# Induced-set attention with a squared-ReLU layer on one core: the first batch's opening redone, and the last batch's second-attention scores made three groups at once

## The chip, the cores and the metric

One core of one Trainium2 chip runs the whole program. The metric is device time in microseconds (us) of one execution; three executions of the kernel before are shown, and their median counts. Engines are named as the profile names them: PE (matmul; PEld is its weight load), DVE, ACT, POOL and SP (which issues the DMAs).

## What is computed

Four batches of 12480 tokens with 128 channels go through a two-step attention over 32 inducing points, and every token's result through a layer of 2048 hidden units. Cut to what matters:

```python
def mab(q, kv):
    s = scale * (q @ kv.transpose(0, 2, 1))
    s = s - s.max(-1, keepdims=True)
    a = np.exp(s)
    a /= a.sum(-1, keepdims=True) + 1e-09
    return a @ kv
h = mab(I, x)            # 32 points look at all tokens of a batch: "scores" and "values"
y = mab(x, h)            # every token looks at the 32 points: "attend"
r = np.maximum(y @ w_in, 0.0)
out = (s * (r * r) + b) @ w_out
```

All inputs are float32 in value; the two weight matrices arrive as float64 and are narrowed on the chip.

## The kernel before

**Units of work.** A block is 480 tokens, a group (`GR`) four blocks; a batch has 26 blocks in seven groups, 0 to 6, the last of two blocks. The hidden layer takes a block in eight pairs of 128 hidden units, so there are 832 pairs in all. `pair` (line 928 its matmuls) makes 256 hidden values for 480 tokens in one of three PSUM buffers `h`: two matmuls, with the second attention folded into the weights `wst` (w_in times h) and the block's attention weights `a2t`. ACT or DVE takes the ReLU (L942, L944), ACT its square rounded to the matmul's short format (`square`, L1010), DVE the exact square (L965), POOL or DVE the remainder (L987). `out_part` (L1035) then multiplies the two pieces with w_out's halves `w_hi` and `w_lo`, six matmuls a pair, into one of two PSUM banks `x`. The first eight pairs (`NATIVE`) instead take the plain float32 square and an unsplit `w_out_raw`: two float32 matmuls a pair.

**Attention beside it.** For each group of four blocks the second attention (`attend`) is one piece on PE (L799: four matmuls that lie side by side in the array), then a transpose, maximum, exponential, sum, product and transpose on DVE and ACT, and DMAs that spread the result into `a2t`. The next batch's first attention is made in the same time: `scores` (L701), `top`, `values` (L742). `visit` puts an `attend` and up to two groups of scores, or a piece of values, into PE's queue one directly behind the other, the scores' results into an `h` buffer; the tables `ATTEND_AT`, `SCORES_WITH`, `VALUES_WITH` and `VALUES_AT` say with which block. In batch 0 before, group 6 of batch 1's scores goes with the first visit, groups 0 to 5 with the next three, and the second piece of batch 1's values stands alone (`VALUES_AT`).

**The opening.** Batch 0's first attention has nothing to hide under. `load_first` brings its tokens (channel by token); `p1_unit` makes the scores (L480), exponential (L493), its transposes (L500) and the values (L511); the tokens that the values need the other way round are made by `turn_x`: eight transposes on PE (L453) and a copy (L214). Only group 5 comes turned from memory (`TURNED`, `load_turned`, 120 rows wide), into a buffer that an earlier group has to free. At the same time eight chunks of weights are loaded (`load_weight`) and narrowed (`narrow`: L331 to L348, five pieces on DVE, two on ACT), and w_out's chunks are split (`split_w_out`, L356). Then the 32 points' values are put together (`h_unit`, `h_out`, L609), the first block's attention is made in a short way (`attend_first`, its last step a cast into `a2t`), `w_first` makes `wst`, and the pairs begin.

**What sets the order.** The program is written by a planner (`Plan`): every step of every unit is a generator's `yield` of an engine, a cost and what it waits for; the planner picks by start time plus a weighted urgency, and the instructions stand in that order in each engine's queue. Constants and tables ahead of the class set it. Each queue runs strictly in order, so a step waits for all that stands ahead of it. The DMAs are all issued by SP, in the order of `ORDER` at first.

Of the kernel before, what the change touches and what calls it, by code (L numbers as in the profile page):

```python
# [19 lines left out]
P = 128  # L20
# [16 lines left out]
SLIP = 0.1744  # L37
WEIGHT = 0.0178
LEAN = {'ACT': -0.5309, 'DVE': 0.6608}
R_LEAN = {'DVE': -0.2301, 'ACT': -0.2128}  # L40


M_U = -5.8018
R_U = 4.5067
SQ = 1.1237
MM = 0.2134
S_U = -0.7565
C_U = -10.6897
OUT_HI = 3.9914
OUT = 0.2122  # L50
FRONT = -1.1612
FIRST = -200.0
SPREAD = 74.0965
FIRST_FRONT = 0.3289
SPLIT_U = 237.6882

NATIVE = 8
H_U = -10.6844
N_U = -24.7788
W_IN_U = -167.7494  # L60
W_OUT_U = 10.3457
W_URGENCY = 3.9038
W_STEP = 19.8754
# [7 lines left out]
RUN = 512  # L71
A_OFF = 19
# [8 lines left out]
TOP_AT = (17, 11, 11)  # L81
VALUES_WITH = (((), (), (), (), (0,), (2, 3)), ((), (), (), (0,), (1,), (2, 3)), ((), (), (), (0,), (1,), (2, 3)))
VALUES_AT = (((1, 20),), (), ())
# [7 lines left out]
VISIT_U = -14.4858  # L91
# [3 lines left out]
class Plan:  # L95
# [7 lines left out]
    def __init__(self):  # L103
        self.free, self.events, self.units, self.end, self.start = {}, {}, [], 0.0, 0.0
        self.eng, self.by = None, {}
# [4 lines left out]
    def _step(self, unit, urgency, ready, src):  # L110
        want = next(unit, None)
        if want is not None:
# [9 lines left out]
            waits = [w for w in waits if not isinstance(w, float) and w != "both"]  # L122
            self.units.append([unit, urgency + more, (ready, src), engs, waits, urgency, lean, None, both])
# [26 lines left out]
    def run(self):  # L150
        while self.units:
            able = {}
            for u in self.units:
# [10 lines left out]
                able.setdefault(eng, []).append((at + WEIGHT * urgency, at, engs[eng], u))  # L164
# [7 lines left out]
            at, _, u, self.eng = min(picks, key=lambda x: x[0])  # L172
            self.units.remove(u)
            self.start, self.end = at, at + u[3][self.eng]
# [7 lines left out]
def tile_attn_relu2(ctx: ExitStack, tc: tile.TileContext, xT, xH, xN, xQ, indT, w_in, w_out, s_rep, b_rep, outT):  # L182
# [13 lines left out]
    const = ctx.enter_context(tc.tile_pool(name="const", bufs=1))  # L196
    xt_pool = ctx.enter_context(tc.tile_pool(name="xt", bufs=XT))
# [13 lines left out]
    def copy(out, in_):  # L211

        if plan.eng == "ACT":
            nc.scalar.copy(out=out, in_=in_)  # L214
        else:
            nc.vector.tensor_copy(out=out, in_=in_)

# [22 lines left out]

    ind_sb = const.tile([P, M], F32, name="ind_sb")
# [5 lines left out]
    w_hi = const.tile([P, NF, P], F32R, name="w_hi")  # L247
    w_lo = const.tile([P, NF, P], F32R, name="w_lo")
# [26 lines left out]
    dma = [2.7]  # L275

    def landing(us, lag=3.0):

        dma[0] = max(dma[0], plan.end + lag) + us * (1.2 if dma[0] < 10.0 else 1.0)
        return dma[0]  # L280
# [4 lines left out]
    def load_xt(gate, b, g, use):  # L285
# [7 lines left out]
        xt_tiles[b, g, use] = t, n  # L293
# [16 lines left out]
    def load_weight(gate, name, c):  # L310
        turn, free = ring("g1", 4)
        yield "SP", 0.45, free, *gate
        sl = slice(c * WC, (c + 1) * WC)
        src, dst = (w_in, w_in_sb) if name == "w_in" else (w_out, w_out_raw.rearrange("p f d -> p (f d)"))
        raw = ew.tile([P, WC, 2], I32, name="g1", bufs=4)
        nc.sync.dma_start(out=raw.rearrange("p n w -> p (n w)"), in_=src[c].bitcast(I32))
        raws[name, c] = raw, turn
        plan.events["raw", name, c] = landing(1.3)
        plan.spawn(narrow((name, c), dst[:, sl], ("raw", name, c)), W_IN_U if name == "w_in" else W_OUT_U)
        if name == "w_out":  # L320
            plan.spawn(split_w_out(c), SPLIT_U)


    def narrow(name, dst, *waits):
        raw, turn = raws.pop(name)
# [15 lines left out]
        nc.vector.scalar_tensor_tensor(out=dst, in0=lo, scalar=2.0**-52, in1=dst, op0=ALU.mult, op1=ALU.add)  # L341
        yield "DVE", 0.62, "both"
# [962 lines left out]
```

## Time and profile before

| | us |
|---|---|
| median of three runs | 1551.88 (1550.89 to 1552.01) |
| the profiled execution, its own time | 1552.4 |
| its span, first to last instruction | 1550.6 |
| PE busy | 1542.8 (99%) |
| POOL busy | 1471.1 (95%) |
| ACT busy | 1482.0 (96%) |
| DVE busy | 1469.9 (95%) |

All four engines are busy nearly all the time, so a share does not tell which one holds the others up. That is read from the chain that ended last (PE has 96% of it), from PE's idle time in each stretch, and, in the opening, from what PE waits for. The profiled execution took 0.5 us more than the median.

### The profile page before, as it was taken

How to read it: one execution, taken by the hardware profiler on the slowest of the kernel's cores; microseconds unless marked ns; L12 is line 12 of the kernel's file. 1: busy time of each engine (PE TensorE's matmuls, PEld its weight loads, DVE VectorE, ACT ScalarE, POOL GpSimd, SP SyncE). 2: the span in 40 equal slices, each digit the busy share in tenths (PEclk: the TensorE clock that was granted, in tenths of full speed). 3: DMA queues.
4: the chain of work that ended last, by engine and by line, in shares of the span. 5: the costliest groups of instructions: out<-in, count | busy, mean ns of one | idle time of the engine just before them, and what ended most of it. 6: DMA issues, size and time to landing. Idle time of an engine off the chain costs nothing.

```text
span 1550.6 us, 24505 instructions
## 1 busy us (share of the span) xinstructions
PE 1542.8 (99%) x8135; PEld 1294.9 (84%) x8135; DVE 1469.9 (95%) x1648; ACT 1482.0 (96%) x1750; POOL 1471.1 (95%) x665
## 2 busy tenths in 40 slices
PE   9999999999999999999999999999999999999999
PEld 6688888888888888888888888888888888888887
DVE  5999999999999999999999999999999999999998
ACT  7899999999999999999999999999999999999998
POOL 0299999999999999999999999999999999999998
PEclk9999999999999999999999999999999999999999
DMA  8212321332233123123232321321313112112100
GB/s 300 64 56 80 122 72 71 114 130 96 68 111 115 39 103 115 39 103 115 71 85 80 118 76 66 115 80 65 112 60 96 32 52 71 40 44 71 57 22 32
DMA packets 53482, 130.12 MB, mean 84 GB/s; under 512 B 11262, under 2 KB 37758, under 8 KB 53358
## 3 DMA queue, kind: packets, MB, share of 16 engines
q1 hardware_dynamic: 53358, 128.56, 25.2%
q8 instruction: 66, 1.08, 0.3%
q14 instruction: 58, 0.48, 0.1%
HBM read 74.50 MB, written 25.56 MB: 65 GB/s over the span
## 4 chain that ended last, share of the span: by engine, by line
PE 96%; DMA 2%; DVE 1%; POOL 0%; issue 0%; ACT 0%; SPq 0%; ACTq 0%; DVEq 0%; POOLq 0%
PE x L1035 68%; PE h L928 23%; PE x L799 2%; PE h L742 1%; PE h L701 1%; DMA g<-in_w_in_dram 1%; DMA xn<-in_xQ_dram 1%; DMA s_sb<-in_s_rep_dram 0%; DVE g L965 0%; POOL g L987 0%; PE h L651 0%; ACT xn L214 0%; PE x L742 0%; PE x L511 0%; SPq L420 0%
## 5 line engine op out<-in xcount | busy, mean ns | idle before, releaser
L987 POOL TENSOR_TENSOR g<-g,g 128x960 fp32r<-128x960 f32 x657 | 1469.8, 2296 | 73.6 <-DVE g L965 67.8
L1035 PE MATMUL x<-g,w_hi 128*128 128x480 f32 x3296 | 1063.6, 375 | 0.0
L1010 ACT ACTIVATE g<-r 128x960 fp32r<-128x960 f32 (+1 forms) x805 | 796.2, 1029 | 16.5 <-DVE r L944 2.4
L965 DVE SCALAR_TENSOR_TENSOR g<-h,r 128x960 f32<-128x960 f32 x657 | 739.4, 1146 | 22.4 <-ACT r L942 14.2
L1035 PEld LDWEIGHTS x<-g,w_hi 128*128 128x128 f32 x3296 | 614.8, 187 | 91.8 <-POOL g L987 3.3
L942 ACT ACTIVATE r<-h 128x960 f32<-128x960 f32 x660 | 622.8, 969 | 27.3 <-PE h L928 26.3
L1035 PE MATMUL x<-g,w_lo 128*128 128x480 f32 x1648 | 617.3, 375 | 0.0
L928 PE MATMUL h<-a2t,wst 128*128 128x480 f32 x1664 | 484.7, 378 | 0.7 <-DVE g L965 0.7
L928 PEld LDWEIGHTS h<-a2t,wst 128*128 128x128 f32 x1664 | 306.6, 187 | 65.4 <-DVE x L805 7.3
L1035 PEld LDWEIGHTS x<-g,w_lo 128*128 128x128 f32 x1648 | 308.9, 187 | 42.8
L944 DVE TENSOR_SCALAR r<-h 128x960 f32<-128x960 f32 x172 | 197.7, 1150 | 9.5 <-PE h L928 7.1
L987 DVE TENSOR_TENSOR g<-h,g 128x960 fp32r<-128x960 f32 x167 | 192.6, 1154 | 12.7 <-ACT g L1010 1.3
L965 DVE SCALAR_TENSOR_TENSOR h<-h,r 128x960 f32<-128x960 f32 x167 | 193.1, 1157 | 6.4 <-ACT r L942 5.7
L1044 ACT ACTIVATE ob<-x,bias 128x480 f32<-128x480 f32 x103 | 68.0, 660 | 4.1 <-PE x L1035 3.9
L799 PE MATMUL x<-xt,hT 128*32 128x480 f32 x208 | 28.3, 578 | 0.0
L805 DVE STREAM_TRANSPOSE x<-x 128x480 f32<-128x480 f32 (+1 forms) x28 | 19.3, 688 | 2.2 <-PE x L799 2.1
L742 PEld LDWEIGHTS h<-xn,eT 128*32 128x32 f32 (+1 forms) x570 | 17.0, 109 | 5.0 <-issue 4.8
L823 DVE STREAM_TRANSPOSE x<-x 128x480 f32<-128x480 f32 (+1 forms) x28 | 19.5, 696 | 0.9
L742 PE MATMUL h<-xn,eT 128*32 128x128 f32 (+1 forms) x570 | 19.6, 273 | 0.0
L821 DVE TENSOR_TENSOR x<-x,l 128x480 f32<-128x480 f32 (+1 forms) x28 | 18.5, 661 | 0.7
L701 PE MATMUL h<-xt,ind_sb 128*32 128x480 f32 x156 | 19.1, 566 | 0.0
L810 DVE TENSOR_TENSOR x<-x,mx 128x480 f32<-128x480 f32 (+1 forms) x28 | 18.4, 656 | 0.1
(147 smaller groups left out, 375.4 us busy)
## 6 DMA issues: line engine op xcount, KB each, us to landing
xt<-in_xT_dram SPq DMA_DIRECT2D x41, 960.0 KB, 5.5
out_dram<-ob SPq DMA_DIRECT2D x104, 240.0 KB, 2.0
a2t<-hl SPq DMA_DIRECT2D x412, 60.0 KB, 2.0
xn<-in_xN_dram SPq DMA_DIRECT2D x18, 512.0 KB, 6.1
xn<-in_xN_dram SPq DMA_DIRECT2D x18, 448.0 KB, 6.7
r<-in_xH_dram SPq DMA_DIRECT2D x7, 480.0 KB, 8.2
xt<-in_xT_dram SPq DMA_DIRECT2D x7, 480.0 KB, 5.4
wst<-hl SPq DMA_DIRECT2D x48, 64.0 KB, 2.0
```

The source lines that it names most:

```text
L701: nc.tensor.matmul(ps[M * q:M * (q + 1), 0:BLK], ind_sb, xt[:, q], start=True, stop=True)
L742: nc.tensor.matmul(ps[M * c:M * (c + 1), 0:P], eT[0:rows, n], xn_tiles[b, g, half][0][0:rows, n - half * TH], start=m < P // M, stop=m + P ...
L799: nc.tensor.matmul(ps[M * q:M * (q + 1), 0:BLK], hT[:, 0:M], xt[:, q], start=True, stop=True)
L823: nc.vector.transpose(out=s, in_=s)
L928: nc.tensor.matmul(h[:, u, 0:BLK], wst[:, c * P:(c + 1) * P], A, start=True, stop=True)
L942: nc.scalar.activation(out=r, in_=hv, func=AF.Relu)
L944: nc.vector.tensor_scalar(out=r, in0=hv, scalar1=0.0, scalar2=None, op0=ALU.max)
L965: nc.vector.scalar_tensor_tensor(out=g, in0=hv, scalar=0.0, in1=r, op0=ALU.max, op1=ALU.mult)
L987: eng.tensor_tensor(out=g2, in0=g, in1=hi.bitcast(F32), op=ALU.subtract)
L1010: nc.scalar.activation(out=q["g1_t"][:, sl, :], in_=q["r_t"][:, sl, :], func=AF.Square)
L1035: nc.tensor.matmul(o, w, g, start=first and n == 0, stop=left == 0 and n == len(ops) - 1)
L1044: nc.scalar.activation(out=ob, in_=o, func=AF.Identity, bias=bias, scale=1.0 if scaled else s_sb)
```

## The change

Batch 0's opening is redone in these ways. Group 6 too comes turned from memory, and both turned groups go to homes of their own (`turned_0` in the second weight tile's room, and the two `hl` buffers), so that their loads wait for nobody; the turned tokens are stored in memory with 128 rows, of which 120 are used. Six token tiles have homes by a table (`X_HOME`). The first super-block comes in two halves. The scores of three groups of batch 1 (6, 4, 5: `GAP`) are made in the opening, after the last values of batch 0, into banks that are free there; the first regular `attend` waits for the evacuation of two of them. w_out's raw chunks get buffers of their own (`w2`), which later hold the split halves in place of `w_hi` and `w_lo`; so the split of a half waits for its raw chunks to be used up, and for `s`, which is now loaded last. Of the narrowing, a piece that ACT did may go to POOL, for three chunks (`POOLED`) a DVE piece is replaced by one on ACT and one on POOL, and the last piece may go to POOL. The order of the loads is new.

The tables of batch 0 follow: the visits there carry scores of groups 0 to 3 only, and its values go with visits as in the other batches. In the last batch `turned_scores` makes the second-attention scores of groups 1, 2, 3 in one visit, and of 4, 5, 6 in another; the extra groups' scores are transposed into an SBUF tile, and their `attend` starts from there, with nothing on PE. All the planner's constants are other ones, and a table of urgencies for single steps (`URGENT`, 55 rows) is added; costs of many steps in the `yield`s are changed by hundredths.

```diff
-SLIP = 0.1744
-WEIGHT = 0.0178
+SLIP = 0.1762
+WEIGHT = 0.0161
...
-TURNED = (5,)
-ORDER = (
-    ("x", 0), ("x", 1), ("w_out", 0), ("x", 2), ("w_out", 1), ("x", 3), ("w_in", 0), ("x", 4), ("w_in", 1),
-    ("w_in", 2), ("x", 5), ("x", 6), ("w_out", 2), ("q", 5), ("w_in", 3), ("w_out", 3),
-)
-WARM = 6
+TURNED = (5, 6)
+X_HOME = (4, 1, 3, 0, 3, 2, 1)
+GAP = (6, 4, 5)
+ORDER = (('x', 0), ('w_in', 1), ('x', 1), ('x', 2), ('w_out', 2), ('w_out', 1), ('w_in', 0), ('w_out', 3), ('x', 3), ('x', 4), ('x', 5), ('x', 6), ('n', 6), ('q', 5), ('w_in', 2), ('q', 6), ('w_in', 3), ('n', 4), ('n', 5), ('w_out', 0), ('s', 0))
+POOLED = (('w_in', 2), ('w_out', 0), ('w_out', 2))
+WARM = 7
+URGENT = {
+    ('x', 3): -234.92,
...
+LAST_WITH = ((2, 3), (), (), (5, 6), (), ())
-SCORES_WITH = (((6,), (0, 1), (2, 3), (4, 5), (), ()), ((0, 1), (2, 3), (4, 5), (), (), ()), ((0, 1), (2, 3), (4, 5), (), (), ()))
+SCORES_WITH = (((), (0, 1), (2, 3), (), (), ()), ((0, 1), (2, 3), (4, 5), (), (), ()), ((0, 1), (2, 3), (4, 5), (), (), ()))
...
-VALUES_WITH = (((), (), (), (), (0,), (2, 3)), ((), (), (), (0,), (1,), (2, 3)), ((), (), (), (0,), (1,), (2, 3)))
-VALUES_AT = (((1, 20),), (), ())
+VALUES_WITH = (((), (), (), (0,), (1,), (2, 3)), ((), (), (), (0,), (1,), (2, 3)), ((), (), (), (0,), (1,), (2, 3)))
+VALUES_AT = ((), (), ())
...
     def load_weight(gate, name, c):
...
+        else:
+            yield "SP", 0.45, *gate
+            raw, used = w2_pool.tile([P, WC, 2], I32, name="w2"), ("raw used", c)
...
     def narrow(name, dst, *waits):
...
-        nc.scalar.activation(out=dst, in_=m, func=AF.Copy, scale=2.0**-20, bias=1.0)
+        yield dict(ACT=0.525, Pool=0.68), {"ACT": M_LEAN}, 0.0
+        if plan.eng == "ACT":
+            nc.scalar.activation(out=dst, in_=m, func=AF.Copy, scale=2.0**-20, bias=1.0)
+        else:
+            nc.gpsimd.tensor_scalar(out=dst, in0=m, scalar1=2.0**-20, scalar2=1.0, op0=ALU.mult, op1=ALU.add)
+        if name in POOLED:
+            yield "ACT", 0.525
+            nc.scalar.activation(out=m.bitcast(F32), in_=lo, func=AF.Copy, scale=2.0**-52)
+            yield "Pool", 1.37
+            nc.gpsimd.tensor_tensor(out=dst, in0=m.bitcast(F32), in1=dst, op=ALU.add)
+        else:
+            yield "DVE", 0.6, "both"
+            nc.vector.scalar_tensor_tensor(out=dst, in0=lo, scalar=2.0**-52, in1=dst, op0=ALU.mult, op1=ALU.add)
...
-        nc.vector.tensor_tensor(out=dst, in0=dst, in1=e.bitcast(F32), op=ALU.mult)
+        yield dict(DVE=0.6, Pool=1.37), 0.0, "both"
+        either().tensor_tensor(out=dst, in0=dst, in1=e.bitcast(F32), op=ALU.mult)
...
     def split_w_out(c):
...
+        yield "ACT", 0.615, "s", ("w_out", c), *[("raw used", n) for n in mine], ("w2", half - 1)
+        if half not in w2:
+            w2[half] = [w2_pool.tile([P, 2 * WC // P, P], F32R, name="w2") for _ in range(2)]
...
     def homes():
...
-            home["x", g] = g if g < 4 else 1 + (g - 4) % 3
+            home["x", g] = X_HOME[g]
...
+        for n in range(SB):
+            home["xQ", TURNED[0] * GR // SB + n] = turned_0[:, n * TH * P:(n + 1) * TH * P]
+        for g in TURNED[1:2]:
+            for n in range(SB):
+                t = p2.tile([P, 2, WC], F32, name="hl")
+                home["xQ", g * GR // SB + n] = t.rearrange("p a t -> p (a t)")
...
     def load_first(g):
...
+            step = SB if j else 1
+            for i in range(0, SB, step):
+                nc.sync.dma_start(out=t[:, a + i:a + i + step].rearrange("p q t -> p (q t)"), in_=xH[j, :, i * BLK:(i + step) * BLK])
...
     def load_turned(g):
...
-            yield "SP", 0.45, ("v done", j - 4)
-            nc.sync.dma_start(out=home["q"][j % 4], in_=xQ[j])
+            yield "SP", 0.45
+            nc.sync.dma_start(out=home["xQ", j], in_=xQ[j])
...
     def scores(b, g, ps, *waits):
...
-                "s": p1.tile([P, NG, BLK], F32, name="s"),
+                "s": st[0]["room"].rearrange("p (g t) -> p g t", g=NG) if b == 1 and GAP
+                else p1.tile([P, NG, BLK], F32, name="s"),
...
+    def turned_scores(b, g, ps, *waits):
+
+        rows = M * blocks_in(g)
+        yield "PE", 1.14, ("hT", b), ("x", b, g, 2), *waits
+        ps = ps()
+        scores_2(b, g, ps)
+        yield "DVE", 0.58
+        nc.vector.transpose(out=st[b]["s"][0:rows, g], in_=ps[0:rows, 0:BLK])
+        plan.set(("turned", b, g))
...
     def attend(b, g, ps, *waits):
...
+        ahead = b == B - 1 and any(g in gs for gs in LAST_WITH)
+        if ahead:
+            yield "DVE", 0.57, ("turned", b, g), *waits
+            ps = ps()
+            s = ps[0:rows, 0:BLK]
+            v = s.rearrange("p (n i) -> p n i", i=M)
+            t = st[b]["s"][0:rows, g].rearrange("p (n i) -> p n i", i=M)
...
     def front_work(blk_g):
...
-                    yield (*want, ("ob", blk_g - 1) if blk_g else "first") if first else want
+                    start = [("ob", blk_g - 1)] if blk_g else ["first", *[("scores", 1, g) for g in GAP[0::2]]]
+                    yield (*want, *start) if first else want
...
-            side = []
+            side = [(turned_scores, b, g) for g in LAST_WITH[n]] if b == B - 1 else []
...
     def opening():
...
-                if n == 1:
-                    nc.sync.dma_start(out=s_sb, in_=s_rep)
-                    nc.sync.dma_start(out=b_sb, in_=b_rep)
...
+            elif what == "n":
+                yield from load_xt((), 1, n, 1)
+                i = GAP.index(n)
+                plan.spawn(
+                    scores(1, n, (lambda: bank[1], lambda: hs[0][:, 0])[i % 2],
+                           ("p1", 0, NG - 1), *([("scores", 1, GAP[i - 2])] if i > 1 else [])),
+                    FIRST + GAP_U + i + urgent("n", n),
+                )
...
 def kernel(x, inducing, moe_w_in, moe_w_out, moe_s, moe_b):
...
+    xq = np.zeros((N // (SB * BLK), P, SB * NQ * C), x.dtype)
+    xq[:, :T] = x[0].reshape(N // (SB * BLK), SB, NQ, T, C).transpose(0, 3, 1, 2, 4).reshape(-1, T, SB * NQ * C)
```

PE's queue where the first pairs begin, before. `accb` with `hl` is the last matmul of the short first attention, `w_in_sb` is `w_first`, `a2t` with `wst` a pair, `hT` the first regular `attend`, `g` with `wst` the first native output piece.

```order
L875 MATMUL x0_85<-accb_101,hl_610 128x120 x4
L632 MATMUL h_114<-w_in_sb_92,hT_575 128x512
L1231 MATMUL h_112<-g2_115 128x320
L928 MATMUL h_627<-a2t_621,wst_587 128x480 x2
L928 MATMUL h_632<-a2t_621,wst_587 128x480 x2
L799 MATMUL x1_86<-xt_117,hT_575 32x480 x4
L928 MATMUL h_645<-a2t_621,wst_587 128x480 x2
L928 MATMUL h_649<-a2t_621,wst_587 128x480 x2
L928 MATMUL h_653<-a2t_621,wst_587 128x480 x2
L1035 MATMUL x0_85<-g_643,wst_111 128x480 x2
```

The same place after; `ind_sb` is a group of batch 1's scores.

```order
L834 MATMUL x1_89<-xt_379,ind_sb_92 32x480 x2
L1031 MATMUL x0_88<-accb_104,hl_614 128x120 x4
L1397 MATMUL h_116<-g2_90 128x480 x2
L1084 MATMUL h_636<-a2t_627,wst_602 128x480 x2
L760 MATMUL h_117<-w_in_sb_97,hT_584 128x512
L760 MATMUL h_118<-w_in_sb_97,hT_584 128x512
L834 MATMUL x1_89<-xt_454,ind_sb_92 32x480 x4
L1084 MATMUL h_659<-a2t_627,wst_602 128x480 x2
L930 MATMUL x1_89<-r_123,hT_584 32x480 x4
L1084 MATMUL h_673<-a2t_627,wst_602 128x480 x2
L1084 MATMUL h_677<-a2t_627,wst_602 128x480 x2
L1084 MATMUL h_683<-a2t_627,wst_602 128x480 x2
L1191 MATMUL x0_88<-g_665,wst_115 128x480 x2
```

Two pieces of `w_first` and one group of scores now stand between the first pair and the second. In both orders five pairs and one `attend` precede the first native output piece.

ACT's queue at the same place, before, from the cast into `a2t` to the first ReLU.

```order
L214 CAST a2t_621<-x0_85 128x480
L214 CAST wst_587<-h_114 128x512
L942 ACTIVATE r_635<-h_627 128x960
```

And after; `w2` with `s_sb` is a w_out chunk's upper half, `rebias` and `g2` are narrowing of the last w_out chunk.

```order
L279 CAST a2t_627<-x0_88 128x480
L458 ACTIVATE w2_632<-wst_115,s_sb_93 128x512 x2
L414 ACTIVATE g_630<-g_630,rebias_108 128x512
L279 CAST wst_602<-h_117 128x512
L422 ACTIVATE g2_639<-w2_457 128x512
L279 CAST wst_602<-h_118 128x512
L1098 ACTIVATE r_657<-h_636 128x960
```

Six pieces stand between the cast into `a2t` and the first ReLU, where one did.

PE's queue at the last batch's first visit of that kind, after; before, a single `attend` of four matmuls stood at each of three such places.

```order
L930 MATMUL x1_89<-xt_12372,hT_11969 32x480 x4
L930 MATMUL h_12658<-xt_12374,hT_11969 32x480 x4
L930 MATMUL h_12658<-xt_12376,hT_11969 32x480 x4
L1084 MATMUL h_12679<-a2t_12291,wst_12076 128x480 x2
```

The second and third group's scores go to an `h` buffer, which a pair would otherwise have.

## Rows read from the trace of the kernel before

**Rows 1.** Page, part 1: busy time, share of the span and instructions.

```profile
PE 1542.8 (99%) x8135; PEld 1294.9 (84%) x8135; DVE 1469.9 (95%) x1648; ACT 1482.0 (96%) x1750; POOL 1471.1 (95%) x665
```

**Rows 2.** Chain that ended last, one piece of it: start us, length us, what.

```profile
74.12 2.13 PE x L1035 x10
```

**Rows 3.** Timeline of PE, 0 to 50 us: start, length, engine, line, operation.

```profile
...
26.65 1.09 PE L453 MATMUL h<-ident,xt 128*120 128x128 f32 x8
27.67 1.01 PE L480 MATMUL x<-r,ind_sb 128*32 128x480 f32 x8
...
29.20 1.00 PE L480 MATMUL x<-r,ind_sb 128*32 128x480 f32 x4
...
35.21 1.74 PE L511 MATMUL x<-xn,eT 120*32 120x128 f32 x44 [1.07 <-DMA xn<-in_xQ_dram]
...
37.51 0.64 PE L609 MATMUL h<-s,sw 128*32 128x128 f32 x14 [0.25 <-DVE rl L595]
...
46.36 1.06 PE L928 MATMUL h<-a2t,wst 128*128 128x480 f32 x4
...
49.75 0.56 PE L1035 MATMUL x<-g,wst 128*128 128x480 f32 x1
```

**Rows 4.** Timeline of PE at five attention pieces in later stretches.

```profile
84.35 1.01 PE L799 MATMUL x<-xt,hT 128*32 128x480 f32 x8
...
86.09 0.70 PE L928 MATMUL h<-a2t,wst 128*128 128x480 f32 x2
...
143.16 1.01 PE L799 MATMUL x<-xt,hT 128*32 128x480 f32 x8
...
145.71 0.70 PE L928 MATMUL h<-a2t,wst 128*128 128x480 f32 x2
...
313.54 1.01 PE L799 MATMUL x<-xt,hT 128*32 128x480 f32 x8
...
316.22 0.69 PE L928 MATMUL h<-a2t,wst 128*128 128x480 f32 x2
...
346.88 0.38 PE L1035 MATMUL x<-g,w_hi 128*128 128x480 f32 x1
347.18 1.94 PE L742 MATMUL x<-xn,eT 128*32 128x128 f32 x60
349.05 0.91 PE L928 MATMUL h<-a2t,wst 128*128 128x480 f32 x3
...
1215.17 1.01 PE L799 MATMUL x<-xt,hT 128*32 128x480 f32 x8
1216.12 0.70 PE L1035 MATMUL x<-g,w_hi 128*128 128x480 f32 x2
```

**Rows 5.** Windows: length; busy PE, PEld, DVE, ACT, POOL; PEclk, DMA share, GB/s.

```profile
5.00:10.00 5.00, 5.00 (x39) 3.09 (x37) 0.81 (x2) 2.63 (x5) 0.00 (x0) 1.00 0.74 242
10.00:15.00 5.00, 4.99 (x60) 2.80 (x56) 1.59 (x4) 4.89 (x10) 0.00 (x0) 1.00 1.01 410
...
30.00:35.00 5.00, 3.86 (x57) 2.87 (x55) 3.82 (x12) 4.65 (x12) 0.00 (x0) 1.00 0.96 237
...
34.00:46.36 12.36, 10.79 (x101) 7.40 (x97) 9.98 (x28) 7.04 (x16) 0.00 (x0) 1.00 0.16 56
```

**Rows 6.** Groups by form, 0 to 46.36 us: busy us, mean ns | idle before.

```profile
L214 ACT COPY xn<-h 120x1024 f32<-120x1024 f32 x11 | 11.3, 1029 | 6.9 <-PE h L453 6.9
...
L637 DVE TENSOR_TENSOR wst<-h,wst 64x512 fp32r<-64x512 f32 x3 | 2.1, 694 | 0.1
...
L356 ACT ACTIVATE w_hi<-wst,s_sb 128x512 fp32r<-128x512 f32 x2 | 1.5, 738 | 0.0
```

**Rows 7.** Timeline of ACT, 45 to 50 us.

```profile
45.48 0.56 ACT L214 CAST a2t<-x 128x480 fp32r<-128x480 f32 x1 [0.33 <-DVE wst L341]
...
47.03 0.97 ACT L942 ACTIVATE r<-h 128x960 f32<-128x960 f32 x1
```

**Rows 8.** Page, part 5: POOL's group.

```profile
L987 POOL TENSOR_TENSOR g<-g,g 128x960 fp32r<-128x960 f32 x657 | 1469.8, 2296 | 73.6 <-DVE g L965 67.8
```

More of the change, by code (lines that the diff above doesn't have):

```diff
@@ new lines @@
+URGENT = {
+    ('x', 3): -234.92,
+    ('w_in', 1): 384.17,
+    ('w', 1): 32.13,
+    ('n', 4): -165.82,
+    ('w', 0): -64.56,
+    ('turn', 4, 0): 27.09,
+    ('turn', 2, 1): 149.29,
+    ('x', 1): 14.97,
+    ('v', 6): 132.81,
+    ('turn', 2, 0): 24.44,
+    ('x', 6): 23.68,
+    ('x', 4): 29.01,
+    ('v', 5): 30.4,
+    ('turn', 0, 0): -1.93,
+    ('turn', 4, 1): 107.18,
+    ('x', 0): 28.8,
+    ('w_in', 3): -107.28,
+    ('w_in', 2): -33.54,
+    ('w_out', 0): 54.0,
+    ('e', 2): -73.1,
+    ('a',): -91.2,
+    ('split', 0): -52.36,
+    ('n', 2): -145.64,
+    ('n', 1): -53.73,
+    ('v', 1): 116.75,
+    ('turn', 6, 1): -158.08,
+    ('n', 6): 31.77,
+    ('turn', 3, 1): -58.68,
+    ('w_out', 1): 2.74,
+    ('w_in', 0): 6.86,
+    ('e', 4): -22.03,
+    ('turn', 1, 0): -1.74,
+    ('split', 1): -56.02,
+    ('turn', 5, 0): -28.41,
+    ('turn', 1, 1): 7.37,
+    ('w_out', 2): -4.46,
+    ('h',): -28.6,
+    ('v', 3): 7.59,
+    ('e', 6): -15.74,
+    ('turn', 5, 1): -19.49,
+    ('n', 3): 5.58,
+    ('split', 3): -0.2,
+    ('x', 2): 0.98,
+    ('n', 5): 1.62,
+    ('n', 0): 40.51,
+    ('turn', 3, 0): 31.87,
+    ('w_out', 3): -50.52,
+    ('e', 3): 27.69,
+    ('w', 3): 59.87,
+    ('w', 2): -21.65,
+    ('e', 5): -27.4,
+    ('e', 1): -29.11,
+    ('v', 4): 3.57,
+    ('e', 0): 0.92,
+}
@@ L121, in _step @@
             more = sum(w for w in waits if isinstance(w, float))
-            waits = [w for w in waits if not isinstance(w, float) and w != "both"]
-            self.units.append([unit, urgency + more, (ready, src), engs, waits, urgency, lean, None, both])
+            kind = True if "tiled" in waits else False if "whole" in waits else None
+            waits = [w for w in waits if not isinstance(w, float) and w not in ("both", "tiled", "whole")]
+            self.units.append([unit, urgency + more, (ready, src), engs, waits, urgency, lean, None, both, kind])
     def extend(self, us):
@@ L392, in homes @@
     def homes():
+        for _ in range(XT):
+            ring("xt", XT)
         for _ in range(2):
-            ring("xt", XT)
             ring("r", 2)
@@ L462, in p1_unit @@
             d = st[0] = {
+                "room": room,
                 "mx": sm.tile([P, NG], F32, name="mx"),
@@ L683, in scores @@
         rows = M * nb
-        if b not in st:
+        if b not in begun:
+            begun.add(b)
+            yield "DVE", 0.15, *waits
             d = st[b] = {
@@ L1034, in out_part @@
         for n, (w, g) in enumerate(ops):
-            nc.tensor.matmul(o, w, g, start=first and n == 0, stop=left == 0 and n == len(ops) - 1)
+            nc.tensor.matmul(o, w(), g, start=first and n == 0, stop=left == 0 and n == len(ops) - 1)
         used()
@@ L1051, in out_part @@
         plan.set(("ob", blk_g))
+    turned_0 = wst_pool.tile([P, F], F32, name="wst")
+    turns = [j for j in range(NSB) if j * SB // GR not in TURNED]
     w_out_raw = wst_pool.tile([P, NF, P], F32, name="wst")
@@ L1169, in tile_attn_relu2 @@
             for f, *args in (args[0], *args[1]) if f is visit else ((f, *args),):
-                if f in (scores, attend):
+                if f in (scores, turned_scores) or f is attend and not any(args[1] in gs for gs in LAST_WITH if args[0] == B - 1):
                     fetch(first + n - AHEAD, load_xt, *args, 1 if f is scores else 2)
@@ L1191, in turn_work @@
         yield from turn_x(g, h, lambda: hs[turns.index(j) % 2], ("turn", before[turns.index(j)]))
-    turns = [j for j in range(NSB) if j * SB // GR not in TURNED]
     before = [-2, -1, *turns]
```

265 lines of the change are left out of this document (154 added, 111 removed).

## Prediction

> **What bounds the kernel now.** I read the page's busy shares first: four engines between 95% and 99% [rows 1], so shares alone settle nothing. The chain that ended last does: after the opening it is PE's own output matmuls, one row after another, and its steps are even, 2.13 us for ten matmuls, so 0.213 us each [rows 2]. From the first pair at 46.36 us [rows 3] to the end PE never waits long for anybody. So in that part a microsecond taken out of PE's queue is a microsecond of the time, and one taken from another engine is worth nothing by itself. Before 46.36 us the picture is another: PE's timeline shows steps of about 1 us each that hang on DMAs and on ACT's copies. The reader should see in the first visit, for example, how a piece of attention stands between two runs of wide matmuls: it starts at 84.35 and the next pair at 86.09 [rows 4]. The difference is its price on PE, and nothing hides it.
>
> So the sum has two terms: by how much PE's regular queue gets shorter, and when it begins. For the second I take the start of the first native output piece, 49.75 us [rows 3], since in both orders the same five pairs and one `attend` stand ahead of it and, but for the first term, the same work behind it.
>
> **Term 1, PE's regular queue.** The prices are distances from an attention piece's start to the next wide matmul [rows 4]: an `attend` alone 1216.12 − 1215.17 = 0.95; with a half group's scores 1.74; with two groups' scores 2.55; with a piece of values 2.68; a piece of values alone 349.05 − 347.18 = 1.87. Each separate piece costs 0.1 more at its entry (347.18 − 346.88 − 0.21 = 0.09). In batch 0, group 6's scores leave the first visit: 1.74 − 0.95 = 0.79 saved. The fourth visit swaps two groups' scores for a piece of values: 0.13 lost. The lone values go into a visit that already existed for the other piece: 1.87 + 0.1 = 1.97 saved. Together 2.6. In the last batch, two times three separate `attend`s of 1.05 (3.15) become one piece of three groups; nearest is 2.55 + 0.1 = 2.65, the same twelve matmuls on the same tiles: 0.5 each, 1.0 together. Term 1 is −3.6 us. The transposes and the maxima that DVE makes for them are as many as before, and lie beside other work; an `h` buffer is held for the time of two transposes, as the visits of the earlier batches hold one, without PE idling there.
>
> **Term 2, the opening.** Three stretches.
>
> *To the products of `h_out` (37.51 us).* Removed from PE are the two transposing steps of group 6; one costs 27.67 − 26.65 = 1.02, so 2.0. The wait of 1.07 us at 35.21 for the turned tokens [rows 3] goes, as their load needs no freed buffer any more, and has 128 rows. In the window from 30 to 35 us, in which the 120-row loads lie, the DMA engines were 96% busy and moved 237 GB/s; from 10 to 15 us 410 [rows 5]. So at most 3.1 us go. At worst nothing goes: ACT's in-order queue makes PE wait instead. I laid the new order's rows behind one another with the distances that the old ones have in the timeline (a copy of turned tokens is 1.03 us [rows 6]). Four weight chunks now load ahead of group 3's tokens, and the copy for group 2's values stands behind four other pieces on ACT; PE waits about 1 us for it, and group 3's scores stand behind that. The last group's scores then start at about 28.8, against 29.20, and the products at 36.8. I take −0.7, near the lower end, since these waits are in the queue whatever PE saves. The DMAs are not what holds this up: by their shapes batch 0's tokens are 6.4 MB, the weights 4.2, the three turned super-blocks 1.6 and the three groups' tokens 2.5, together 14.7; with the 1.2 MB of 5 to 10 us (242 GB/s) and 410 GB/s from then on [rows 5] the last weight chunk and `s` are there by 43 us, and they are needed at about 45.
>
> *To the cast into `a2t` (45.48 [rows 7]).* Now 7.97 us. One `w_first` subtraction on DVE, 0.694 [rows 6], that stood in the chain of the first block's softmax is behind it now. −0.7, so the cast comes at about 44.1. The scores of groups 4 and 6 fill PE's place where warming matmuls stood: nothing.
>
> *From the cast to the first native output piece.* Now 4.27 us; ACT's first ReLU starts 1.55 after the cast [rows 7]. Six pieces stand between in the new order where one cast did: two upper halves (0.738 each [rows 6]), two narrowing pieces of about that size and two casts; with their overlap the five more are some 3 us. PE has two `w_first` and a group's scores behind the first pair, and the regular `attend` must wait until DVE has emptied that group's bank, which stands behind two `w_first` subtractions and a split. The fifth pair needs the buffer that the second ReLU empties. Bounds: 4.3 if all of it found room, 4.3 + 4.3 if ACT's five pieces, a split and a subtraction on DVE all added up. I take 7.5, near the upper end, since the two queues block each other in order and only part of the added pieces can overlap. The first native piece then starts at 51.6: 1.85 us later than now, though the first pair starts 1.4 earlier. The two `w_first` and the scores are not lost: the scores are what term 1 no longer pays.
>
> **Sum.** +1.85 − 3.6 = −1.75 us. Against the profiled execution's 1552.4 that is 1550.65; that one was 0.5 over the median, so **1550.1** for the median of 1551.88. What a measurement of this kernel can tell from no change is about 0.2%, 3.1 us, so the forecast is "within".
>
> **Rivals.** *The opening keeps what it saves.* If ACT's five pieces find room while the casts wait for `w_first` anyway, the last stretch is as now and the first native piece comes at 44.1 + 4.3 = 48.4, 1.35 earlier: −1.35 − 3.6 = −4.95, 1546.9 us. If the 3.1 us of the first stretch come in full as well, 1544.5. For it: PE had 1.1 us of plain DMA wait, two steps of it go, and ACT loses 2 copies of 1.03. Against: the in-order waits above.
>
> *POOL's narrowing holds DVE.* Twelve pieces of narrowing stand on POOL now, where it was idle until the pairs (its idle time before L987 is 73.6 us [rows 8]); six of them after the last scores. None is in the trace; by L987, 2.296 us for 960 columns, one of 512 would take 1.22. If DVE's pieces of the same time stand still for each, that is 7.3 us of which DVE, 10.0 us busy of the 12.4 before the pairs [rows 5], can hide 2. The first native piece comes at 56.9: +7.15 − 3.6 = +3.55, 1555.4 us, slower. It decides from 53.35 on (the sum is then zero) and is slower by over 0.2% from 56.5. In the steady part POOL and DVE work at once without it, but there a DVE piece takes one input from PSUM. The Trainium skill, "SBUF — State Buffer", section Who interferes with whom, speaks against the change here: VectorE and GpSimd share a port pair as an exclusive lock, and "a DVE instruction with two SBUF inputs contends with a GpSimd instruction that reads SBUF"; narrowing has both. By that rule DVE's narrowing and POOL's would take turns. No row of now has the two side by side, so it stays a rival with a small chance, as only pieces that meet in the last 10 us cost anything.
>
> *The order made anew.* Every constant of the planner is another one, and all 832 pairs are put in another order. PE has almost nothing to win there [rows 2] and can lose: 4.9 us more, or 0.047 us a block over 104 blocks, turn the forecast into slower by 0.2%, 1555.
>
> **How the numbers follow.** The forecast (first native piece between 50.1 and 56.4) 0.48; the opening that keeps its savings 0.36; POOL's hold on DVE 0.11; the order made anew 0.05. Faster by over 0.2%: 0.36; within: 0.48; slower: 0.16. The range runs from 1545.5, the first rival with part of the 3.1 us, to 1554.0, the forecast with the upper ends of the last stretch and some of DVE's waits; beyond it lie the rest of both slower rivals and the best case of the first. The likeliest case's own range is 1548.8 to 1553.5.
>
> **What would show it.** Right: the last scores near 29, the first pair near 45, the first native output piece near 51.6, ACT's first ReLU some 4 us after the cast into `a2t`; single `attend`s of 0.95 where there were 1.74 and 2.55, two pieces of three groups at about 2.6 in the last batch, no lone values. Wrong in the first way: that native piece before 50. Wrong in the second: narrowing pieces on DVE well over 0.7 us beside POOL's. Wrong in the third: a PE idle column that is no longer near zero after 70 us.

## The result, and the profile after

The changed kernel takes **1562.97 us** (median of 5 runs, 1560.7 to 1564.21), the kernel before 1551.88 in the same job (five runs, 1550.89 to 1555.36, three of which stand ahead): ratio 1.0068, 95% interval 1.0057 to 1.0079. It is slower by 11.1 us, far outside the noise; forecast were 1550.1 us and no change beyond 0.2%.

The profiled execution took 1560.7 us. From its page, the busy shares and two of the costliest groups:

```profile
span 1558.9 us, 24450 instructions
...
PE 1548.0 (99%) x8123; PEld 1302.1 (84%) x8123; DVE 1478.8 (95%) x1655; ACT 1472.4 (94%) x1729; POOL 1474.4 (95%) x674
...
L1191 PE MATMUL x<-g,w 128*128 128x480 f32 x4944 | 1191.5, 377 | 0.5 <-DVE hl L986 0.5
...
L1084 PE MATMUL h<-a2t,wst 128*128 128x480 f32 x1664 | 487.0, 378 | 0.1
```

PE waits for nobody: 0.5 us in 1500. The granted clock was 1.00 in this execution and in that of before, the level of 2.4 GHz, so the clock has no part in it. All the same PE is busy longer than before [rows 1]. Where that comes from shows when one piece of its queue is laid beside the same piece of a kernel in which the split weights lie elsewhere and all else is in the same order (e1 below). PE's timeline of the changed kernel, then that of e1:

```profile
302.64 0.59 PE L1084 MATMUL h<-a2t,wst 128*128 128x480 f32 x2
303.07 1.46 PE L1191 MATMUL x<-g,w 128*128 128x480 f32 x6
...
304.80 2.33 PE L1191 MATMUL x<-g,w 128*128 128x480 f32 x10
306.96 0.59 PE L1084 MATMUL h<-a2t,wst 128*128 128x480 f32 x2
...
313.87 0.38 PE L1084 MATMUL h<-a2t,wst 128*128 128x480 f32 x1
```
```profile
301.88 0.59 PE L1085 MATMUL h<-a2t,wst 128*128 128x480 f32 x2
302.31 1.44 PE L1192 MATMUL x<-g,w 128*128 128x480 f32 x6
...
304.01 2.29 PE L1192 MATMUL x<-g,w 128*128 128x480 f32 x10
306.15 0.59 PE L1085 MATMUL h<-a2t,wst 128*128 128x480 f32 x2
...
312.97 0.59 PE L1085 MATMUL h<-a2t,wst 128*128 128x480 f32 x2
```

The same 52 matmuls take 313.87 − 302.64 = 11.23 us here and 312.97 − 301.88 = 11.09 there: 0.2160 against 0.2133 us each. Ten output matmuls take 306.96 − 304.80 = 2.16, against 2.14 there and 2.13 before [rows 2]. No wait shows; the steps themselves are longer. They are not so everywhere. Two pieces of the changed kernel's own chain, ten output matmuls each, read weights and tiles at the same offsets:

```profile
304.96 2.17 PE x L1191 x10
...
329.31 2.13 PE x L1191 x10
```

Most stretches between two pieces of attention have a mean of 0.2159 us a step, a few have the old 0.2134 (from 964 to 1018 us, for example). So the place, as the experiments below show, makes the slow pace possible; what decides between the two paces from stretch to stretch is open. Over the whole trace after 68 us, the mean distance between the starts of neighbouring wide matmuls, steps with a wait left out, is 0.2134 us before and 0.2152 after. In 6516 of them that makes **11.7 us**.

The sum from the first native output piece to the last matmul: 1546.73 − 49.75 = 1496.98 us before and 1554.84 − 52.74 = 1502.10 after, 5.1 more. The pieces of attention give 3.55, PE's long steps (over 0.233 us, as far as they are over the regular 0.2133) fall from 14.7 to 11.9 us in all and give 2.8, and the pace takes 11.7: 5.3, near enough. The other 3.0 lie in the opening, on the way to that first native piece. Together 8.1 us. The rest of the 11.1 is the choice of executions: the profiled one is 2.3 under its median, that of before 0.5 over its own.

The opening after, PE's timeline, with the wait that was new:

```profile
44.51 0.70 PE L1084 MATMUL h<-a2t,wst 128*128 128x480 f32 x2
...
48.53 0.70 PE L1084 MATMUL h<-a2t,wst 128*128 128x480 f32 x2
50.41 1.01 PE L930 MATMUL x<-r,hT 128*32 128x480 f32 x8 [1.18 <-DVE s L837]
...
52.74 1.79 PE L1191 MATMUL x<-g,wst 128*128 128x480 f32 x4
```

and what DVE and POOL did ahead of that wait:

```profile
47.92 1.74 DVE L460 SCALAR_TENSOR_TENSOR w<-wst,s_sb,w 128x512 fp32r<-128x512 f32 x1
49.69 0.66 DVE L837 TENSOR_SCALAR_CACHE_REDUCE s<-x 128x480 f32<-128x480 f32 x1
```
```profile
47.81 1.29 POOL L424 TENSOR_TENSOR wst<-g,wst 128x512 f32<-128x512 f32 x1 [1.42 <-ACT g L422]
```

DVE's split of a weight chunk (the lower half; the 0.738 of [rows 6] is ACT's upper half) took 0.741 before:

```profile
L358 DVE SCALAR_TENSOR_TENSOR w_lo<-wst,s_sb,w_hi 128x512 fp32r<-128x512 f32 x1 | 0.7, 741 | 0.0
```

Now it takes 1.74 while POOL adds beside it, and the maxima that PE waits for (L837) stand right behind.

### The profile page after: what moved, and what is told of

It reads as the page before. It is cut to its first block, busy times and chain, and to the rows that moved or that the text cites. A ratio compares the mean times of both kernels' runs of the same rounds, so it can differ in the third digit from the quotient of the medians.

```text
span 1558.9 us, 24450 instructions
## 1 busy us (share of the span) xinstructions
PE 1548.0 (99%) x8123; PEld 1302.1 (84%) x8123; DVE 1478.8 (95%) x1655; ACT 1472.4 (94%) x1729; POOL 1474.4 (95%) x674
## 4 chain that ended last, share of the span: by engine, by line
PE 97%; ACT 1%; DVE 1%; DMA 0%; issue 0%; POOL 0%; SPq 0%; ACTq 0%; DVEq 0%; POOLq 0%
PE x L1191 69%; PE h L1084 23%; PE x L930 1%; PE h L875 1%; PE h L834 1%; PE h L577 0%; ACT g L1166 0%; DMA g<-in_w_in_dram 0%; PE x L637 0%; ACT r L1098 0%; PE x L605 0%; PE h L930 0%; PE h L779 0%; POOL g L1143 0%; DVE g L1121 0%
## 5 line engine op out<-in xcount | busy, mean ns | idle before, releaser
L1191 PE MATMUL x<-g,w 128*128 128x480 f32 x4944 | 1191.5, 377 | 0.5 <-DVE hl L986 0.5
L1191 PEld LDWEIGHTS x<-g,w 128*128 128x128 f32 x4944 | 928.0, 188 | 137.6 <-DVE hl L986 1.3
L1098 ACT ACTIVATE r<-h 128x960 f32<-128x960 f32 x654 | 616.2, 968 | 43.5 <-PE h L1084 40.4
L1084 PEld LDWEIGHTS h<-a2t,wst 128*128 128x128 f32 x1664 | 310.0, 188 | 61.8 <-issue 6.6
L1100 DVE TENSOR_SCALAR r<-h 128x960 f32<-128x960 f32 x178 | 204.7, 1150 | 14.0 <-PE h L1084 12.4
L1143 DVE TENSOR_TENSOR g<-h,g 128x960 fp32r<-128x960 f32 x169 | 194.9, 1153 | 11.1 <-DVE h L1121 0.5
L930 PE MATMUL x<-xt,hT 128*32 128x480 f32 x172 | 23.2, 578 | 0.0
L970 DVE TENSOR_REDUCE x<-x 128x15 f32<-128x480 f32 (+1 forms) x28 | 18.3, 655 | 0.7 <-ACT x L968 0.6
L986 DVE TENSOR_TENSOR hl<-x,hl 128x480 fp32r<-128x480 f32 (+1 forms) x28 | 17.9, 641 | 0.1
```

Source lines behind the costliest of these rows:

```text
L930: nc.tensor.matmul(ps[M * q:M * (q + 1), 0:BLK], hT[:, 0:M], xt[:, q], start=True, stop=True)
L1084: nc.tensor.matmul(h[:, u, 0:BLK], wst[:, c * P:(c + 1) * P], A, start=True, stop=True)
L1098: nc.scalar.activation(out=r, in_=hv, func=AF.Relu)
L1100: nc.vector.tensor_scalar(out=r, in0=hv, scalar1=0.0, scalar2=None, op0=ALU.max)
L1143: eng.tensor_tensor(out=g2, in0=g, in1=hi.bitcast(F32), op=ALU.subtract)
L1191: nc.tensor.matmul(o, w(), g, start=first and n == 0, stop=left == 0 and n == len(ops) - 1)
```

## Experiments

In the kernel before, `w_hi` and `w_lo` lie at bytes 9024 and 17216 of each partition, right behind `w_in_sb`. The change takes them out of the pool of constants, and its four tiles `w2` lie behind that pool at 10240, 14336, 18432 and 22528. The moving tiles (those that stream through PE while the weights stay in it) of the pairs, of the output and of the regular attention lie where they did, and so does `wst`. The old places of the weights have offset 320 within 512 bytes, the new ones 0; the output's moving tiles begin at 460. The code pieces of this section are shortened.

**e1, e2: the place alone.** e1, in the changed kernel:

```diff
     const = ctx.enter_context(tc.tile_pool(name="const", bufs=1))
     w2_pool = ctx.enter_context(tc.tile_pool(name="w2", bufs=4))
+    const2 = ctx.enter_context(tc.tile_pool(name="const2", bufs=1))
-    bias, ident, ones, rebias, sel = const.tile(...)
+    bias, ident, ones, rebias, sel = const2.tile(...)
```

> The changed kernel, with the four tiles of the split output weights at the places in SBUF that they had before the change (9024 to 25407 instead of 10240 to 26623 in each partition, the small constants behind them); every instruction and every engine's order is that of the changed kernel. Theory A (the place of the weights in SBUF sets the pace of the output matmuls, each second of which starts 217.6 ns after the one ahead of it instead of 213.6): the mean start to start of PE's steady matmuls goes back from 0.2152 to 0.2134 us, and with some 6500 of them the time falls by 11.7 us, to 1551.3 us (1549.5 to 1553). Theory B (the planner's new order of units on PE, DVE and ACT sets the pace): nothing moves, 1563 us (1561 to 1564.5), pace 0.2152 us. Theory C (the two halves in tiles of their own, written and waited for apart, cost it): as B, nothing moves.

e2, in the kernel before:

```diff
-    w_hi, w_lo = const.tile(...)      # behind w_in_sb
     sel = const.tile([P, P], F32, name="sel")
+    w_hi, w_lo = const.tile(...)
```

> The kernel before, with w_hi and w_lo allotted last among the constants, so that they lie at 10240 and 18432 instead of 9024 and 17216; the instructions and every engine's order are those of the kernel before. Theory A (place of the weights): the pace goes from 0.2134 to about 0.2152 us and the time rises by some 11.7 us, to 1563.5 us (1560 to 1565). Theory B (the planner's order) and theory C (tiles of their own): nothing moves, 1551.9 us (1550.5 to 1553.5).

Measured: e1 **1551.15 us**, 0.9997 of before (0.9988 to 1.0006), pace (mean step of PE's wide matmuls) 0.2134. e2 **1561.79 us**, 1.0064 (1.0051 to 1.0076), pace 0.2154. Ten output matmuls in e2's chain, 2.13 in the kernel before [rows 2]:

```profile
303.01 2.17 PE x L1035 x10
```

Moving the weights takes the loss out of one kernel and puts it into the other. Theories B and C fall. Five small constants change places with the weights in both runs; e8 below leaves both where they were.

**e3, e4: other places.** Quarters of the weights, each at another offset:

```diff
-    w_hi = const.tile([P, NF, P], F32R, name="w_hi")
-    w_lo = const.tile([P, NF, P], F32R, name="w_lo")
+    w_hi[0], w_lo[0] = const.tile([P, WC // P, P], ...), const.tile(...)
+    s_sb = const.tile([P, 1], F32, name="s_sb")
+    w_hi[1], w_lo[1] = ...
...
```

> The kernel before, with w_hi and w_lo cut into four quarters of 2 KB a partition (blocks 0-3, 4-7, 8-11, 12-15 of the hidden dimension), high and low of a quarter side by side, and small constants between the quarters, so that their byte offsets within 512 are 128, 160, 192 and 224; instructions and order as before. The output matmuls of each quarter are read apart. Theory A1 (weights that begin at a multiple of 512 bytes are slow, all else is fast): 0.2134 us a matmul in all four, time 1551.9 us (1550.5 to 1553.5). Theory A2 (it depends on where the weights lie against the moving tile, which begins at offset 460 of 512): some quarters fast, some slow by up to 0.004 us for every second matmul, time between 1552 and 1563 us.

> As the run before it, with the quarters at offsets 256, 288, 448 and 0 within 512 bytes. Theory A1: only the fourth quarter (offset 0) is slow, each second of its matmuls by 0.004 us; a quarter of some 10 to 11.7 us, so about 1554.5 us. Theory A2: the fourth quarter is slow and one or more of the others too, 1554 to 1563 us. If no quarter is slow, it was the distance between high and low part (8192 bytes there, 2048 here), and neither holds: 1551.9 us.

Measured 1552.85 and 1561.89 us (e3, e4, e5, e8, e9 and e10 are one execution each). Steps onto a new moving tile within a quarter, mean: 0.2134 us at 128, 160 and 224, 0.2146 at 192; 0.2167 at 256, 0.2155 at 288, 0.2145 at 448, 0.2170 at 0. So 0 is not the only slow place: A1 falls, A2 stands. A slow neighbour is felt elsewhere too: between the two matmuls of a pair, whose tiles kept their places, the step went from 0.2135 to 0.2144 us.

**e5, e8: the moving tile shifted instead.** `G_OFF = 3` becomes 19 in both kernels.

> The changed kernel, weights at its own places (multiples of 512 bytes), with the moving tiles of the output matmuls 64 bytes further on (G_OFF 19 words instead of 3: offset 12 within 512 instead of 460); order the same. Theory A1 (the weights' own place): no change, 1563 us and 0.2152 us a matmul. Theory A2 (weights against moving tile): the pace changes, either way, by over 0.0005 us a matmul, 3 us or more of the time.

> The kernel before, weights at its own places (offset 320 within 512 bytes), with the moving tiles of the output matmuls 64 bytes further on (offset 12 instead of 460); order the same. Theory R (what counts is the distance between weights and moving tile, modulo 256 bytes: 52 in the changed kernel, slow; 116 before, fast): the distance becomes 308, so 52 modulo 256, as in the changed kernel: 1562 us (1559 to 1566) and 0.2150 us a matmul or more. Theory W (the weights' own place alone, 0 and 256 slow): no change, 1552 us, 0.2134 us.

Measured: e5 1568.79 us, pace 0.2165, so A1 falls here too; e8 **1561.73 us**, pace 0.2153. In e8's chain:

```profile
303.54 2.17 PE x L1035 x10
```

The kernel before becomes as slow as the changed one with its weights untouched, as theory R forecast for this place; theory W falls. In e5 the matmuls that keep the moving tile and take new weights became slow too (0.2182 us).

**e9, e10: PE alone, and beside the others.** The loop of both:

```python
for at in (460, 12, 76, 140):            # offset of the moving tile
    for step in range(0, 512, 32):       # offset of the weights
        nc.tensor.matmul(o[0][:, 0:128], w[:, 0:P], m[:, 0:128], ...)
        for n in range(64):
            nc.tensor.matmul(o[1][:, 0:480], w[...], m[...], ...)
```

> No attention: PE alone. 4096 matmuls of the output's form (weights 128x128, moving tile 480 columns, low and high weights 8192 bytes apart in turn, a new moving tile at every second one), all on constant tiles, in 64 groups of 64: weights at offsets 0, 32, ... 480 within 512 bytes, for moving tiles at offsets 460, 12, 76 and 140; all other engines idle; the output is not computed. Theory P (PE's own reads of weights and of the moving tile meet): groups differ as in the kernels, 0.2134 us a matmul in some, 0.2155 us and more in others. Theory C (reads and writes of the other engines are needed): 0.2134 us in all groups.

> As e9, with the other engines at work beside PE, on tiles of their own: POOL 390 subtractions of 960 columns, DVE 780 of its pieces, ACT 860 squares; nothing waits for PE or is waited for; the output is not computed. Theory P: the groups' paces are those of e9. Theory C: groups differ here, 0.2134 us in some and 0.2155 us and more in others, and not in e9.

PE's timeline of e9, the groups with the moving tile at 460 and weights at 0 and 32, then with the tile at 76 and weights at 0; a single small matmul parts the groups:

```profile
22.35 14.08 PE L59 MATMUL o<-m,w 128*128 128x480 f32 x64
36.26 0.22 PE L54 MATMUL o<-m,w 128*128 128x128 f32 x1
36.33 13.88 PE L59 MATMUL o<-m,w 128*128 128x480 f32 x64
50.04 0.22 PE L54 MATMUL o<-m,w 128*128 128x128 f32 x1
...
465.56 13.88 PE L59 MATMUL o<-m,w 128*128 128x480 f32 x64
479.29 0.22 PE L54 MATMUL o<-m,w 128*128 128x128 f32 x1
```

(36.26 − 22.35) / 64 = 0.2173 us, (50.04 − 36.33) / 64 = 0.2142, (479.29 − 465.56) / 64 = 0.2145: the same weights are slow with one moving tile and fast with another. By the starts in ns (the rows are rounded to 0.01 us) all 64 groups fall into two kinds, 0.2141 to 0.2144 and 0.2174 to 0.2176 us a step. The slow ones (weights at x and at x + 256 have the same pace, to 0.0002 us):

| moving tile at | weights slow at, and 256 further on |
|---|---|
| 460 (as in both kernels) | 0, 96, 192 |
| 12 | 0, 64, 160 |
| 76 | 224 |
| 140 | 32, 192 |

The distance from tile to weights, modulo 256, is 52, 148 or 244 in every slow group, though not every group with such a distance is slow: with the tile at 76 and weights at 128 it is 52, and that group is fast. So theory R, the distance alone, falls as a rule. In e10 the groups' paces are the same to 0.0001 us, with DVE, ACT and POOL at work. Between the groups only the two addresses differ, so it lies in PE's own two reads, of the weights and of the moving tile: theory P holds, theory C falls. The table gives the right sign for both kernels, e2, e5 and e8, but not for all of e4: weights at 288 were slow there (0.2155), and 32 is fast in e9.

e10 shows something else as well. Its groups of instructions, first while POOL works, then when POOL is done:

```profile
L55 DVE SCALAR_TENSOR_TENSOR g<-g,g 128x960 f32<-128x960 f32 x255 | 795.4, 3119 | 8.7
L53 POOL TENSOR_TENSOR g<-g,g 128x960 f32<-128x960 f32 x255 | 784.1, 3075 | 20.0
```
```profile
L55 DVE SCALAR_TENSOR_TENSOR g<-g,g 128x960 f32<-128x960 f32 x336 | 389.5, 1159 | 11.7
```

DVE's piece with both inputs in SBUF takes 1.16 us alone and 3.12 beside POOL's, with 255 of each in the same 800 us: one by one, so the two take turns.

**e6, e7: the last batch's half by itself.** e6 puts `LAST_WITH` with `turned_scores` into the kernel before; e7 takes it out of e1:

```diff
-LAST_WITH = ((2, 3), (), (), (5, 6), (), ())
+LAST_WITH = ((),) * 6
```

> The kernel before, everything as it was up to the last batch (opening, weights' places, planner's constants), with the second half of the change alone: in the last batch the attention scores of groups 2 and 3, and of 5 and 6, made in one piece with those of group 1 and 4. By the prediction's first term PE's queue is 1.0 us shorter (two times three separate pieces of 1.05 become one of about 2.65), nothing else moves: 1550.9 us (1549.8 to 1551.8). Rival: what the pieces save is given back at their place, since DVE has two transposes more in a row there: 1551.9 us or over.

> The changed kernel with its weights at the places of before (as e1), and without the second half of the change: in the last batch each attend makes its own scores again; the opening and batch 0 are the changed ones, the planner's constants are the changed ones, and up to the last batch the order is that of e1. By the prediction's first term the last batch's pieces cost 1.0 us more: 1552.1 us (1551.5 to 1553.3) against e1's 1551.15. Rival (the other half alone lost 2.8 us in e6 because its plan lets PE run out of work in the last batch): what the half is worth depends on the plan; then this is at or below 1551.2 us.

e6: **1554.36 us**, 1.0018 (1.0009 to 1.0027): slower by 2.6. Its attention pieces are cheaper, but by 0.56 us where 1.0 was expected (68.73 us in all, 69.29 before), and PE's long steps rise from 14.7 to 18.2 us, nearly all of it in the last batch (from 1200 us on 2.9 before, 6.2 here). One of them in PE's timeline:

```profile
1451.72 0.48 PE L1059 MATMUL x<-g,w_hi 128*128 128x480 f32 x1 [0.90 <-POOL g L1011]
```

In the kernel before, PE waits for nobody from 1380 us on. e7: 1552.10 us, 0.95 over e1's median; set each against its own runs of before (0.9999, 0.9997) only 0.3. The trace has 0.88 us more in its attention pieces. So in the changed kernel's order the half is worth 0.9 us by the trace; the times, with intervals of about 1.4 us either way, agree with that but do not show it. In an order made with the old constants it costs 2.6, and that is clear of the noise.

**e11, e12: the piece that held DVE.** e11, in e1's kernel, makes the last chunk's addition on DVE, two pieces later:

```diff
-            nc.gpsimd.tensor_tensor(out=dst, in0=m.bitcast(F32), in1=dst, op=ALU.add)
+            if name != ("w_out", 0):
+                nc.gpsimd.tensor_tensor(out=dst, in0=m.bitcast(F32), in1=dst, op=ALU.add)
...
         yield "DVE", 0.6, "both"
+        if name == ("w_out", 0):
+            nc.vector.tensor_tensor(out=dst, in0=m.bitcast(F32), in1=dst, op=ALU.add)
```

> As e1 (the changed kernel, weights at the places of before), but for one piece of the opening: the pooled addition of the last chunk of w_out (512 columns, two inputs in SBUF) is made by DVE, behind the maxima of the last score group and a w_first subtraction, instead of by POOL beside DVE's split of another chunk; all other rows keep their order. In the changed kernel that split took 1.74 us where before it took 0.74, and behind it stood the maxima for which PE waited. Theory: POOL's piece held DVE; the split takes 0.74 again, the first regular attend starts 1.0 earlier, and so does everything behind it: 1550.1 us (1549.3 to 1551). Rival: the split was slow for a reason of its own, or PE's wait is taken over by ACT's casts and ReLUs: 1551.2 us.

e12, in e1's kernel, `POOLED = (('w_in', 2), ('w_out', 2))`.

> As e1, with that chunk taken off the list of those whose addition POOL makes (POOLED), so that the planner makes a new order from there on; one native output piece now stands ahead of the first regular attend. Theory (the opening's gain carries through): as the run before it or a little better, 1549 to 1550.5 us. Rival (an order made anew has waits of its own, as in e6): 1552 to 1554 us, with PE waits of over 2 us in all after 100 us.

e11, DVE's timeline and PE's:

```profile
49.12 0.75 DVE L464 SCALAR_TENSOR_TENSOR w<-wst,s_sb,w 128x512 fp32r<-128x512 f32 x1
```
```profile
45.71 0.70 PE L1088 MATMUL h<-a2t,wst 128*128 128x480 f32 x2
...
50.62 1.01 PE L934 MATMUL x<-r,hT 128*32 128x480 f32 x8 [0.19 <-DVE s L841]
...
53.40 1.88 PE L1195 MATMUL x<-g,wst 128*128 128x480 f32 x4 [0.28 <-DVE wst L439]
```

The split takes 0.75 again, and the `attend` comes 4.91 us behind the first pair, not 5.9. But the first native piece comes 7.69 behind it, not 8.24: half of the gain turns into a wait for the last chunk's narrowing, which is now later on DVE. The time is **1550.84 us**, 0.9993 of before (0.9984 to 1.0002): the lowest median here, not told apart from before nor from e1. That POOL's piece held the split is shown; a gain in time is not.

e12: **1566.84 us**, 1.0097 (1.0082 to 1.0113). Its first native piece is early (50.34) and its pace is 0.2134, but PE's long steps add up to 30.1 us, where e1 has 13.7. PE's waits after 100 us, e12's two longest and then e1's:

```profile
PE h L1085 <- DVE g L1122: 3.9, 9, 1.1
PE x L1192 <- DVE hl L987: 0.7, 3, 0.3
```
```profile
PE x L1192 <- DVE hl L987: 0.7, 2, 0.4
```

All of e12's waits from 100 to 1550 us come to 5.0 us; the rest of its long steps has no wait in the view. Both times forecast for e12 were missed; the rival's sign, over 2 us of waits, came. One entry of a list, and the order of everything behind it costs 15.7 us against e1.

## Why the prediction was wrong

**Step that failed.** Term 2 took the first native output piece as the mark, since behind it stood, "but for the first term, the same work"; with [rows 2] that meant 0.213 us a matmul as before. A change of that pace stood in the sum at nothing, without a reason. The work is the same, the pace is not: 0.2152 us, 11.7 us in all. I had read the tile pools of the change for who waits for which buffer, and never for where the buffers lie. e1 and e2 show that this is the whole loss, to within e1's interval of about 1.4 us either way.

**Term 1 held.** Attention pieces of the steady part fell by 3.55 us, where 3.6 was forecast. The first piece of three groups, in PE's timeline after:

```profile
1223.50 1.01 PE L930 MATMUL x<-xt,hT 128*32 128x480 f32 x8
1224.33 1.79 PE L930 MATMUL h<-xt,hT 128*32 128x480 f32 x16
1226.05 0.70 PE L1084 MATMUL h<-a2t,wst 128*128 128x480 f32 x2
```

1226.05 − 1223.50 = 2.55, the price taken from [rows 4].

**Term 2 was mis-sized.** PE's timeline after, then ACT's:

```profile
35.92 0.30 PE L737 MATMUL h<-s,sw 128*32 128x128 f32 x2
```
```profile
43.89 0.56 ACT L279 CAST a2t<-x 128x480 fp32r<-128x480 f32 x1 [0.80 <-PE x L1031]
...
48.18 0.98 ACT L1098 ACTIVATE r<-h 128x960 f32<-128x960 f32 x1
```

`h_out` came at 35.92 (forecast 36.8), the cast into `a2t` at 43.89 (44.1), ACT's first ReLU 4.29 behind it (some 4). From the cast to the first native piece 8.85 us passed, where I took 7.5. One microsecond of delay in it is the split that POOL held, though e11 won back only half of it. The mark came 2.99 later than before, not 1.85. Between executions that varies: with the old opening the first pair starts anywhere from 44.99 to 46.36 us (six kernels' traces, before the latest of them), with the new one from 44.50 to 45.71 (five). From pair to native piece it is always 3.4 with the old and 8.2 with the new one, but for the 7.69 of e11. By the means of the six and of the four without e11 the mark moved from 49.02 to 52.93, 3.9 later: the term was short by 2 us.

**The sum, with the weights mended**, is −3.55 + 2.99 = −0.56 us; e1 measures 1551.15 against 1551.72 in its job, −0.57. That they agree so closely is luck: the 2.99 is the distance of two single executions, and the long steps are left out. In e1's own trace:

```profile
45.17 0.70 PE L1085 MATMUL h<-a2t,wst 128*128 128x480 f32 x2
...
53.41 1.80 PE L1192 MATMUL x<-g,wst 128*128 128x480 f32 x4
```

Its mark is 3.66 later than the 49.75 of before, and from there to the last matmul it takes 1545.32 − 53.41 = 1491.91 us, 5.07 less (pieces 3.6, long steps 1.0, the rest not split up): −1.4, against an execution of before that was 0.5 over its median. By its interval, −1.9 to +0.9 us, e1 can be told neither from no change nor from the forecast −1.75.

**The rivals.** *The opening keeps what it saves*: no. *POOL's narrowing holds DVE*: it happened, for 1.0 us on the way to PE's wait, not for 7.3. Three narrowing pieces of DVE too, at 18.63, 19.32 and 20.69 us, took 0.77, 0.83 and 1.10 us beside POOL's where the same pieces take 0.43, 0.41 and 0.68; what those cost is not shown. The Trainium skill, "SBUF — State Buffer", section Who interferes with whom, has the rule, and e10's 3.12 against 1.16 us agrees with it. *The order made anew*: its sign, PE waits after 70 us, did not come in the changed kernel; but e6 and e12 show that it decides in other orders of this same program, with 2.6 and 15.7 us, so it was dismissed too lightly as a mechanism.

No rival was about where a tile lies. The same section of the Trainium skill says "PE and ACT never wait on anyone"; for PE beside other engines e10 agrees, with the paces of e9 to 0.0001 us. The Trainium skill, "TensorE: Matmul & The Clock Gate", section Step-by-step: what each phase is for, says that loading the next weights takes no read bandwidth from the running matmul. By that rule the place of the weights should not matter; e9, 0.2173 against 0.2142 us with every other engine idle, differs, and the measurement decides.

## What to carry to other kernels

When a change adds, drops or moves a tile pool, compare the addresses of what PE reads, before and after, not only the order of its instructions. Where PE is the bound and never waits, read the distance between the starts of neighbouring matmuls first, over the whole trace: 2.13 us for ten [rows 2] against 2.16 after was all that showed, and not in every stretch. And a part that shortens PE's queue in one planned order can lose in another: the same half takes 0.9 us off the queue in e7's comparison, by the trace alone, and costs 2.6 us in e6.

## What the runs showed of the hardware, unexpected

- PE's pace depends on where the weights lie against the moving tile: 0.2141 to 0.2144 us or 0.2174 to 0.2176 us a matmul of 480 columns in e9, repeating every 256 bytes of the weights' place, the same with the other engines idle or at work (e10). Why at distances of 52, 148 and 244, and why not in every group with them, stays open, as does how a slow step reaches matmuls whose tiles kept their places (e3 to e5), and why the changed kernel runs some stretches at 0.2134 and most at 0.2159 with the same places.
- DVE with two SBUF inputs and POOL take turns, held for unlikely to matter here: 1.16 us becomes 3.12 (960 columns), 0.75 becomes 1.74 (512 columns). In the opening two DVE pieces with one input (L409, L412) were longer beside POOL's as well, 0.77 and 0.83 us for 0.43 and 0.41; that was seen there only, not tested.
